# All FFN1 pairs of a parallel attention and FFN block take their last 64 features as stacks that pass DRAM

## The chip, the cores and the metric

One core of a Trainium2 chip runs the whole kernel. The metric is device time in microseconds (us) of one execution; lower is better. TensorE (PE) multiplies, VectorE (DVE) and ScalarE (ACT) work on the tiles between, GpSimd (POOL) does little arithmetic but issues loads and stores, and SyncE (SP) issues most of the other transfers. Each engine works through its own instructions in order; an instruction that must wait for data holds up everything behind it on the same engine.

## The reference

The input `x` has 2048 tokens of 576 features. Attention and FFN both read it and their results are added:

```python
def _A_ref(x, wqkv, wo):            # H = 32 heads of Dh = 18
    qkv = (x @ wqkv).reshape(B, S, 3, H, Dh)...
    idx = pos[:, None] - (jnp.arange(8) * 2)[None, :]      # 8 keys, every second token back
    logits = jnp.einsum("bhsd,bhswd->bhsw", q, kg) * Dh ** -0.5
    attn = softmax(where(idx >= 0, logits, -1e9))
    return einsum("bhsw,bhswd->bhsd", attn, vg)... @ wo
...
def _B_ref(x, w1, b1, w2, b2):      # F = 4608
    h = jnp.einsum("bsd,df->bsf", x, w1) + b1
    h = jnp.square(jax.nn.relu(h))
    return jnp.einsum("bsf,fd->bsd", h, w2) + b2
...
out = x + attention(layernorm(x)) + ffn(layernorm(x))
```

Everything is fp32. The kernel multiplies in PE's `fp32r` format and keeps fp32 accuracy by splitting each operand in a high part (ACT copies it, rounding) and a low part (DVE subtracts), and adding the three products high x high, low x high and high x low.

## The kernel before

The tokens are four blocks of 512, the FFN width is 36 tiles of 128, taken as 18 *pairs* (`p`). The first half (`s` = 0) does blocks 0 and 1, the second half (`s` = 1) blocks 2 and 3. A pair of FFN tiles against a pair of blocks is a 2 x 2 product, done as seven block products in the manner of Winograd: B11, T1, T2, T3, B21, B22 and T4 (`product` in `ffn_pair`). Each is six matmuls of 128 x 128 by 128 x 512 over the first 512 features: two chunks of 128, each with the three split products. `w1s` holds the split weights of a pair in two tiles (k = 0 and 1) with four product slots each; `combine_w1` makes T1, T2 and T4 weights on DVE, `w1_hi` and `w1_lo` split them in the first half and store them in DRAM (`w<-w1s`), and `w1_again` loads them back in the second half.

The last 64 features are treated apart, in one of two ways:

- *Unstacked* (`left`): the 64 features' high rows and low rows lie in one tile of 128 rows (`x4`), and two matmuls at four places of the pair add them, 8 a pair. All 18 pairs of the first half and pairs 0 and 1 of the second half do that. It needs a weight slot of its own, `LEFT`, the eighth in `w1s`.
- *Stacked*: the 64 features are two halves of 32 that go through the same seven products. High, low and high rows of a half lie on 96 partitions, beside weight rows high, high and low, so one matmul per product does all three split products: 7 a pair. Pairs 2 to 17 of the second half do that. Their weights are made per pair from a 256 KB load (`mb<-in_w1l`) by `left_weight_sums`, `left_weight_hi` and `left_weight_lo`; the stacks themselves are built on DVE and ACT while pairs 1 and 2 of the second half run (`stack_sums`, `stack_hi`, `one_stack` and their like).

The phases are: the QKV matmuls of blocks 0 and 1 (`q0`), the 18 pairs of the first half (`phase_a(0)`), a bridge of FFN2 work and the QKV of blocks 2 and 3 in 2 x 2 steps called quads (`phase_b0`), the 18 pairs of the second half (`phase_a(1)`), and the end (`phase_b1`). Within a pair, FFN2 matmuls of the pair before (L536) stand between the products. PE order in a pair: B11, T1, T2, T3, B21, B22, T4. `bc`, `ba`, `bb` are its three PSUM banks; T1 and later B22 go to `bc`, and B22 may start there once DVE has added T1's result to T3's (`r1[:, 1] = bc + u[:, 1]`).

Attention of each block runs on DVE in steps beside the pairs. `side(k)` takes up to k steps at a fixed place of the pair: after T1 three or so, after B22 two, after T4 two. A block and group (`b`, `g`) needs keys and queries, then values: keys and values are loads of 1296 KB into one of three `kv` tiles. `offer` lists the loads, `fetch` issues the next as long as a tile is free (`free`, less `kept_back` that it may not touch), and `release` gives a tile back, after the last `pr<-q,kv` for keys and after the last `q<-pr` for values. They are issued on POOL, in its order with the eight stores of a finished group (`o<-q`). The statistics of blocks 2 and 3 (`statistics`, L135 and the small operations behind it) are steps too; their input takes a `kv` tile, and they end with a store of 4 KB (`mr<-mr`) on SP.

In a pair, SP issues a store of r1 of the pair before (`h<-r`), two loads of w2 (`w2r<-in_w`) and between them a store of split w1, then in the first half a load of raw w1 (`w1r<-in_w`) for two pairs on. Each of these waits for the DVE instruction that frees its tile or makes its data.

## Time and profile before

| What | Value |
|---|---|
| Median of 3 runs | 1107.31 us (1107.31 to 1108.32) |
| The profiled execution | 1107.93 us, of which the span is 1106.2 us |
| QKV of blocks 0 and 1 | up to about 92 us |
| First half's pairs | from 92 to about 411 us, one every 17.68 us |
| FFN2, QKV of blocks 2 and 3 | to about 630 us |
| Second half's pairs | from 630 to about 952 us, one every 17.45 us where stacked |
| Bytes moved by DMA | 287.83 MB, 260 GB/s on average |

An execution outside the profile's span costs 1.7 us here. Busy time of an engine counts only if something else waits for it. In a row of the timeline the numbers are the start, the duration, the engine, the line, the operation, out<-in, and, in brackets, the time that the engine was idle just before and what ended that. In a row of transfers the last number is the median time from issue to landing. Chain lines give start, duration, engine, tile, line and the number of instructions merged.

### The profile page before, as it was taken

To read this page: it belongs to the slowest core of one execution; us is meant where nothing else is said; L and a number is where in the kernel's file an instruction comes from. 1 tells how busy PE (TensorE), PEld (TensorE's weight loads), DVE (VectorE), ACT (ScalarE), POOL (GpSimd) and SP (SyncE) were. 2 spreads that over 40 slices of the span, in tenths; PEclk is the share of its full clock that TensorE was granted. 3 is DMA by queue.
4 is the path that set the end of the run, shared out by engine and by line. 5 is a ranking of instruction groups with operands and counts; after the bars stand their busy time and mean duration, and the time that the engine had idled before them with its cause. 6 is when DMAs were issued, how large, how long until landed. Compare 5 with 4: busy or idle time off the path is not lost.

```text
span 1106.2 us, 13892 instructions
## 1 busy us (share of the span) xinstructions
PE 1096.8 (99%) x4950; PEld 925.2 (84%) x4950; DVE 912.0 (82%) x1223; ACT 575.0 (52%) x809; POOL 115.4 (10%) x219
## 2 busy tenths in 40 slices
PE   9999999999999999999999999999999999999998
PEld 7998888888888888888899887888888888888887
DVE  7696979897996979999979488978988789899654
ACT  5435666556566654455344355555555555533342
POOL 4000101020020100100010200202102021000100
PEclk9999999999999999999999999999999999999999
DMA  8956987889699686866755887768686785866752
GB/s 297 329 177 234 333 309 255 296 214 372 229 244 392 220 357 214 311 247 226 259 164 169 309 263 300 259 260 308 238 315 240 267 314 205 316 208 205 280 193 81
DMA packets 100279, 287.83 MB, mean 260 GB/s; under 512 B 13288, under 2 KB 41712, under 8 KB 85488
## 3 DMA queue, kind: packets, MB, share of 16 engines
q1 hardware_dynamic: 65280, 188.15, 49.1%
q0 software_dynamic: 10544, 52.14, 12.9%
q10 hardware_dynamic: 24384, 46.64, 12.6%
q8 instruction: 39, 0.64, 0.2%
q14 instruction: 32, 0.26, 0.1%
HBM read 205.14 MB, written 81.74 MB: 259 GB/s over the span
## 4 chain that ended last, share of the span: by engine, by line
PE 89%; DVE 5%; DMA 3%; ACT 1%; issue 1%; ACTq 0%; POOL 0%; DVEq 0%; POOLq 0%; SPq 0%
PE p L536 46%; PE p L629 31%; PE p L1041 5%; PE p L635 3%; DMA kvq<-st 2%; PE p L338 1%; PE p L1401 1%; PE p L1045 1%; DVE pr L108 1%; DMA kv<-kvq 1%; DVE lg L387 1%; DVE w1r L108 1%; DVE r L108 0%; PE p L1318 0%; DVE h L108 0%
## 5 line engine op out<-in xcount | busy, mean ns | idle before, releaser
L536 PE MATMUL p<-h,w2s 128*128 128x512 f32 x2066 | 491.4, 389 | 0.1
L536 PEld LDWEIGHTS p<-h,w2s 128*128 128x128 f32 x2066 | 387.5, 188 | 81.5 <-ACT h L642 0.6
L629 PE MATMUL p<-X,w1s 128*128 128x512 f32 x864 | 219.7, 389 | 1.2 <-DVE r L108 0.9
L629 PEld LDWEIGHTS p<-X,w1s 128*128 128x128 f32 x864 | 162.0, 188 | 35.6 <-DVE r L108 1.3
L509 ACT ACTIVATE w2s<-w2r 128x640 fp32r<-128x640 f32 x164 | 120.2, 735 | 116.1 <-PE p L536 87.6
L629 PE MATMUL p<-S,w1s 128*128 128x512 f32 x648 | 164.8, 390 | 1.5 <-ACT r L691 1.5
L108 DVE TENSOR_TENSOR w2s<-w2r,w2s 128x576 fp32r<-128x576 f32 x164 | 123.4, 753 | 40.6 <-ACT w2s L509 39.8
L629 PEld LDWEIGHTS p<-S,w1s 128*128 128x128 f32 x648 | 121.4, 188 | 27.4 <-ACT r L691 2.3
L415 POOL DMA_DIRECT2D o<-q x128 | 69.2, 605 | 584.8 <-DVE q L108 582.8
L638 ACT ACTIVATE r<-r,b1t 128x512 f32<-128x512 f32 x72 | 52.0, 723 | 126.9 <-DVE r L108 125.2
L387 DVE TENSOR_REDUCE lg<-pr 128x64 f32<-128x1152 f32 x64 | 86.5, 1352 | 1.5
L108 DVE TENSOR_TENSOR pr<-lg,kv 128x1152 f32<-128x1152 f32 x64 | 86.7, 1354 | 1.3
L108 DVE TENSOR_TENSOR pr<-q,kv 128x1152 f32<-128x1152 f32 x64 | 86.6, 1353 | 0.8
L108 DVE TENSOR_TENSOR pr<-pr 128x576 f32<-128x576 f32 (+1 forms) x128 | 77.5, 605 | 3.2
L646 ACT ACTIVATE r<-r 128x1024 f32<-128x1024 f32 x72 | 76.1, 1057 | 1.2
L108 DVE TENSOR_TENSOR h<-r,h 128x1024 fp32r<-128x1024 f32 (+3 forms) x46 | 51.8, 1136 | 27.0 <-ACT r L646 18.8
L108 DVE TENSOR_TENSOR r<-p,r 128x512 f32<-128x512 f32 (+1 forms) x77 | 52.9, 688 | 20.3 <-PE p L629 9.8
L108 DVE TENSOR_TENSOR w1s<-w1r,w1s 128x1024 fp32r<-128x1024 f32 (+1 forms) x42 | 50.3, 1198 | 16.5 <-ACT w1s L477 16.4
L691 ACT ACTIVATE r<-p 128x512 f32<-128x512 f32 x36 | 21.5, 597 | 70.9 <-PE p L629 70.5
L638 ACT ACTIVATE r<-p,b1t 128x512 f32<-128x512 f32 x72 | 48.3, 672 | 0.0
L108 DVE TENSOR_TENSOR h<-h 128x1024 fp32r<-128x1024 f32 x36 | 43.9, 1220 | 4.8 <-ACT h L938 4.6
L536 PE MATMUL p<-w1s,w2s 128*128 128x512 f32 x195 | 44.7, 389 | 0.0
(193 smaller groups left out, 1174.2 us busy)
## 6 DMA issues: line engine op xcount, KB each, us to landing
w2r<-in_w SPq DMA_DIRECT2D x144, 320.0 KB, 3.4
kv<-kvq POOLq DMA_DIRECT2D x29, 1296.0 KB, 9.4
w<-w1s SPq DMA_DIRECT2D x36, 1024.0 KB, 8.4
w1s<-w ACTq DMA_DIRECT2D x34, 1024.0 KB, 7.3
h<-r SPq DMA_DIRECT2D x36, 512.0 KB, 6.3
h<-h SPq DMA_DIRECT2D x36, 512.0 KB, 4.2
w1r<-in_w SPq DMA_DIRECT2D x18, 640.0 KB, 7.7
kvq<-st ACTq DMA_DIRECT2D x48, 216.0 KB, 3.2
```

The lines of the kernel that those rows point to most:

```text
L108: return nc.vector.tensor_tensor(out=out, in0=a, in1=b, op=op)
L338: nc.tensor.matmul(p[:, :QW], l, r, start=k == 0, stop=k == len(mm) - 1)
L387: nc.vector.tensor_reduce(out=lg[:, j * HG:(j + 1) * HG].rearrange("p a w -> p w a"), in_=pr.rearrange("p w (a d) -> p w a d", d=DH), axis ...
L415: nc.gpsimd.dma_start(rows[:, i], q[i * L:(i + 1) * L, :, a:z])
L509: nc.scalar.activation(w2s[stream[i]][:, :DE], raw2[i], AF.Copy)
L536: nc.tensor.matmul(yp[b][c], v, a, start=c not in yb[b], stop=c in last and c not in [o[0] for o in ops[i + 1:]], skip_group_check=True)
L629: nc.tensor.matmul(to, l, r, start=start and i == 0, stop=i == len(mm) - 1, skip_group_check=True)
L635: nc.tensor.matmul(to, weight(LEFT, k, f), v, start=False, stop=k == 1, skip_group_check=True)
L638: nc.scalar.activation(to, a, AF.Relu, bias=b1t[:, f:f + 1])
L646: nc.scalar.activation(r, r, AF.Square)
L691: nc.scalar.activation(u[:, 0], bb, AF.Copy)
L1041: nc.tensor.matmul(to, l[:, js], r, start=start and n == 0, stop=n == len(mm) - 1, skip_group_check=True)
```

## The change

All 36 pairs use the stacked form. `left` and the `LEFT` weight slot go, and the second w1 tile has three slots instead of four. The first half gets stacks as well (`left_x(0)`), and those of the second half are built earlier, while `phase_b0` runs. Building goes over all 128 partitions at once: four groups of 32 rows are four quarters of a block's tokens (`left_x`) or four pairs' weights (`left_w`). A high and a low version of 128 x 896 are made by one ACT and one DVE operation (`split_rows`), and twelve stores of 32 x 896 put them in the order of the stacks into DRAM, from where `load_stacks` fetches the stacks once a half and `load_left_weights(p + 1)` a pair's weights in every pair, behind T3.

The stack of the first half stays in one of the three `kv` tiles (with two small tiles beside it) until its pairs are done; `free` and `kept_back` are set for that. In the first pair of the second half, one row of quad output is stored later than before (`held`), behind the copy of T2's bank. In the first half `side` has other counts. The diff, cut to its core:

```diff
-T1, T3, B11, T2, B22, B21, LEFT, T4 = range(8)
+T1, T3, B11, T2, B22, B21, T4, LEFT = range(8)
 B12 = T2
 OA, OB = 3 * L, CG - 3 * L
+K3 = 3 * L
+NS = 7
+STACK = {T1: 0, B11: 1, B22: 2, B21: 3, T3: 4, T2: 5, T4: 6}
...
-    w1scr = [[dram.tile([P, 16 * P], F32, name=f"w1{p}{k}") for k in range(2)] for p in range(NP)]
-    xlscr = {b: dram.tile([2 * L, TB], F32, name=f"xl{b}") for b in (2, 3)}
+    w1scr = [[dram.tile([P, 2, 4 - k, 2 * P], F32, name=f"w1{p}{k}") for k in range(2)] for p in range(NP)]
+    xlscr = [dram.tile([2 * L, TB], F32, name=f"xl{b}") for b in range(NB)]
+    stscr = [dram.tile([K3, NS, TB], F32, name=f"stk{s}") for s in range(2)]
+    lwscr = [dram.tile([K3, NS * P], F32, name=f"lw{p}") for p in range(NP)]
...
+        if s == 0:
+            return
...
-        raw1[n] = sb.tile([P, 8, 2 * P], F32, name="w1r", bufs=2)
-        nc.sync.dma_start(raw1[n][:, B11:LEFT + 1], w1[n % NP])
+        raw1[n] = sb.tile([P, NS, 2 * P], F32, name="w1r", bufs=2)
+        nc.sync.dma_start(raw1[n][:, B11:B21 + 1], w1[n])
...
+    def open_w1(n, k):
+        w1s[n, k] = mt.tile([P, 2, 4, 2 * P], F32R, name="w1s", bufs=3)[:, :, :4 - k]
+        return w1s[n, k]
...
-    def open_left_weights():
-        t = sb.tile([P, 2, 7, P], F32R, name="w1r", bufs=2)
-        LW[0], LW[1] = t[:, 0], t[:, 1]
...
-    def left_weight_hi(p):
-        nc.scalar.activation(LW[p % 2], LR["w"], AF.Copy)
-    def left_weight_lo(p):
-        rows = slice(2 * L, P)
-        tt(LW[p % 2][rows], LR["w"][rows], LW[p % 2][rows].bitcast(F32), ALU.subtract)
-        load_left_weights(p + 1)
...
+    def split_rows(v, order, out):
+        lo, hi = v[:, :NS], v[:, NS:]
+        yield
+        nc.scalar.activation(hi.bitcast(F32R), lo, AF.Copy)
+        yield
+        tt(lo.bitcast(F32R), lo, hi, ALU.subtract)
+        for g in range(G):
+            for k, part in enumerate(order):
+                to = out(g, slice(k * L, (k + 1) * L))
+                if to is not None:
+                    nc.sync.dma_start(to, (hi, lo)[part][g * L:(g + 1) * L])
+        yield
...
+    def left_x(s):
+        v = rv.pop(s)
+        x = lambda k: v[:, STACK[k]]
+        tt(x(T3), x(B11), x(T1), ALU.subtract)
+        tt(x(T1), x(T1), x(T4), ALU.add)
+        tt(x(T2), x(T1), x(B11), ALU.subtract)
+        tt(x(B22), x(B21), x(T2), ALU.subtract)
+        yield from split_rows(v, (0, 1, 0), lambda g, rows: stscr[s][rows, :, g * P:(g + 1) * P])
+    def load_stacks(s, *tiles):
+        i = 0
+        for t in tiles:
+            n = min(t.shape[1], NS - i)
+            nc.sync.dma_start(t[:K3, :n].bitcast(F32), stscr[s][:, i:i + n])
+            for k, place in STACK.items():
+                if i <= place < i + n:
+                    ST[k] = t[:K3, place - i]
+            i += n
...
+    def left_w(i):
+        v = rv.pop(("w", i))
+        w = lambda k: v[:, STACK[k]]
+        tt(w(T3), w(B22), w(T1), ALU.subtract)
+        tt(w(T1), w(T1), w(B11), ALU.subtract)
+        tt(w(T2), w(B22), w(T1), ALU.subtract)
+        tt(w(T4), w(B21), w(T2), ALU.subtract)
+        yield from split_rows(v, (0, 0, 1), lambda g, rows: lwscr[G * i + g][rows].rearrange("r (s c) -> r s c", c=P)
+                              if G * i + g < NP else None)
...
     def load_left_weights(p):
-        if p < NP:
-            nc.sync.dma_start(LR["w"][:, 2:6], w1l[p])
-    def left_weight_sums():
-        r = LR["w"]
-        tt(r[:, 0:2], r[:, 3:5], r[:, 2:4], ALU.subtract)
-        tt(r[:, 3], r[:, 4], r[:, 0], ALU.subtract)
-        tt(r[:, 6], r[:, 5], r[:, 3], ALU.subtract)
-    def left_weight_hi(p):
-        nc.scalar.activation(LW[p % 2], LR["w"], AF.Copy)
-    def left_weight_lo(p):
-        rows = slice(2 * L, P)
-        tt(LW[p % 2][rows], LR["w"][rows], LW[p % 2][rows].bitcast(F32), ALU.subtract)
-        load_left_weights(p + 1)
+        src = lwscr[p].rearrange("r (s c) -> r s c", c=P)
+        tiles = ([sb.tile([P, NS, P], F32R, name="mb")] if p % 2 == 0 else
+                 [mt.tile([P, 4, P], F32R, name="x40"), mt.tile([P, 4, P], F32R, name="x41")])
+        i = 0
+        for t in tiles:
+            n = min(t.shape[1], NS - i)
+            nc.sync.dma_start(t[:K3, :n].bitcast(F32), src[:, i:i + n])
+            for k, place in STACK.items():
+                if i <= place < i + n:
+                    LW[p % 2, k] = t[:K3, place - i]
+            i += n
...
-            if stacked:
-                mm.append((LW[p % 2][:, STACK[slot]], ST[slot]))
+            mm.append((LW[p % 2, slot], ST[slot]))
...
-        def left(to, f, v):
-            if stacked:
+        def part(i):
+            if s:
                 return
-            for k in range(2):
-                nc.tensor.matmul(to, weight(LEFT, k, f), v, start=False, stop=k == 1, skip_group_check=True)
+            r = p // G + 1
+            if i == 0 and p % G == 1 and G * r < NP:
+                load_left_w(r, sb.tile([P, 2 * NS, P], F32, name="st"))
+            elif p % G == 2 and G * r < NP:
+                if i == 0:
+                    rv["of", r] = left_w(r)
+                next(rv["of", r])
...
+        part(0)
         if not first:
-            side(1 if p == 1 else 3 if s else 2 + p % 2, s == 1)
+            side(2 if not s and p % 4 == 2 else 3, s == 1)
...
         product(bb, T3, ss(3))
-        if first:
-            left(bc, 1, x4[b1])
+        if not last:
+            load_left_weights(p + 1)
...
             product(bc, B22, S4)
-            left(bc, 1, x4["d"])
-            if s and p == 1:
-                left_weight_lo(2)
-                one_stack_lo(T2)
-            elif not first:
+            part(1)
+            if not first:
                 side(2)
...
+        else:
+            release()
+            load_xf(2)
...
+            put = lambda: row_out(n, f, x, y)
+            held.append(put) if held is not None else put()
+        def row_out(n, f, x, y):
...
+                if (s, i) == (1, 0):
+                    load_stacks(1, *(sb.tile([P, 4, TB], F32R, name="w1r", bufs=2) for _ in range(2)))
+                    load_left_weights(0)
...
+        held = []
         def filler(i):
-            if i < 2:
-                quads(1, 1, [len(steps) - 2 + i])
+            if i == 0:
+                quads(1, 1, [len(steps) - 2], held)
+            if i == 0.5:
+                held.pop()()
             if i == 1:
-                load_left_rows()
-                LR["w"] = sb.tile([P, 7, P], F32, name="mb")
-                load_left_weights(2)
+                quads(1, 1, [len(steps) - 1])
...
+                free[0] -= 1
+                kept_back[0] = 0
+                load_left_x(0, kv_tile(2 * NS * P).rearrange("p (s t) -> p s t", t=P))
+            if r == 13:
+                load_left_weights(0)
...
+                load_stacks(0, sb.tile([P, 5, TB], F32R, name="kv", bufs=3), mt.tile([P, 1, TB], F32R, name="x4d"),
+                            sb.tile([P, 1, TB], F32R, name="xf"))
...
+    kept_back[0] = 1
```

**POOL, from the end of attention of block 0, group 3, to the next one's loads (around pair 8 of the first half).** `kv<-kvq_98` loads keys and later values of the next group, `q<-kvq_98` its queries, `o_100` and `o_101` are the outputs of the finished group, `mr` are the statistics of block 2. Before:

```order
L358 DMA q<-kvq_98 128x576
L360 DMA kv<-kvq_98 128x2592
L415 DMA o_100<-q 128x1x96 x4
L415 DMA o_101<-q 128x1x48 x4
L360 DMA kv<-kvq_98 128x2592
L144 TENSOR_TENSOR mr<-mr,half 128x1 x4
```

Now:

```order
L425 DMA o_100<-q 128x1x96 x4
L425 DMA o_101<-q 128x1x48 x4
L368 DMA q<-kvq_98 128x576
L370 DMA kv<-kvq_98 128x2592
L149 TENSOR_TENSOR mr<-mr,half 128x1 x4
L370 DMA kv<-kvq_98 128x2592
```

The loads of queries and keys stood ahead of the eight output stores and now stand behind them.

**DVE, at the end of block 2's statistics in the same pair.** `w2s`, `w1s` are weight splits, `r<-p,r` with the lower tile is the add that frees the bank for B22, `pr<-q,kv` the next group's first product with keys. Before:

```order
L135 BN_STATS st_2216<-kv 128x6 x2
L139 BN_AGGR mv<-st_2216 128x2
L158 COPY mr<-mv 128x1
L143 TENSOR_SCALAR mr<-mv 128x1
L108 TENSOR_TENSOR w2s<-w2r,w2s 128x576
L108 TENSOR_TENSOR w1s<-w1r,w1s 128x1024
L108 TENSOR_TENSOR w2s<-w2r,w2s 128x576
L108 TENSOR_TENSOR r_2274<-p_2189,r_2242 128x512
L108 TENSOR_TENSOR w1s<-w1r,w1s 128x1024
L108 TENSOR_TENSOR pr<-q,kv 128x1152
```

Now:

```order
L140 BN_STATS st_2347<-kv 128x6 x2
L144 BN_AGGR mv<-st_2347 128x2
L163 COPY mr<-mv 128x1
L148 TENSOR_SCALAR mr<-mv 128x1
L113 TENSOR_TENSOR pr<-q,kv 128x1152
L113 TENSOR_TENSOR w2s<-w2r,w2s 128x576
L113 TENSOR_TENSOR w1s<-w1r,w1s 128x1024
L113 TENSOR_TENSOR w2s<-w2r,w2s 128x576
L113 TENSOR_TENSOR r_2414<-p_2318,r_2379 128x512
L113 TENSOR_TENSOR w1s<-w1r,w1s 128x768
```

The product with the new keys has moved ahead of the weight splits and of the add, by five places.

**SP, from the store of block 2's statistics (`mr_109`) on, in the same pair.** `h_178` and its like are stores of r1, `w_129` of split w1, and `x_2408`, `x_2409` are the two tiles that take the left weights of pair 9 from DRAM. Before:

```order
L162 DMA mr_109<-mr 128x8x1
L150 DMA kv<-in_x 128x2304
L656 DMA h_156<-r_2101 128x1024
L499 DMA w2r<-in_w 128x640
L483 DMA w_129<-w1s 128x2048
L499 DMA w2r<-in_w 128x640
L467 DMA w1r<-in_w 128x1280
```

Now:

```order
L167 DMA mr_109<-mr 128x8x1
L682 DMA h_178<-r_2231 128x1024
L511 DMA w2r<-in_w 128x640
L496 DMA w_129<-w1s 128x2048
L511 DMA w2r<-in_w 128x640
L619 DMA x_2408<-lw_162 96x512
L619 DMA x_2409<-lw_162 96x384
L477 DMA w1r<-in_w 128x1024
```

The load of block 3's rows (`kv<-in_x`) has left this place, since no `kv` tile is free for it there; the two loads of left weights have come in behind the second w2r.

118 lines of the change are left out of this document (37 added, 81 removed).

## The prediction

> **What bounds the kernel now.** I read the page first: busy time, then the chain that ended last.
>
> ```profile
> PE 1096.8 (99%) x4950; PEld 925.2 (84%) x4950; DVE 912.0 (82%) x1223; ACT 575.0 (52%) x809; POOL 115.4 (10%) x219
> PE 89%; DVE 5%; DMA 3%; ACT 1%; issue 1%; ACTq 0%; POOL 0%; DVEq 0%; POOLq 0%; SPq 0%
> ```
>
> PE is busy 99% of the span and carries 89% of the chain. So a matmul less is time won, and any other engine costs time only where it makes PE wait. Next I read the chain in order of time inside the pair loop, at the same matmuls of successive pairs: two lines from the first half, two from the second.
>
> ```profile
> 118.37 2.72 PE p L629 x12
> 136.05 2.72 PE p L629 x12
> 759.81 3.17 PE p L629 x14
> 777.26 3.17 PE p L629 x14
> ```
>
> Twelve matmuls take 2.72 us, 0.227 each. The pair takes 17.68 us in the first half and 17.45 in the second: the difference is one matmul, 8 unstacked against 7 stacked ones for the last 64 features. PE never rests inside such a pair, so it is the limit there. Last came PE's waits, for the little that is not matmul.
>
> **Matmuls removed.** The list of PE groups by shape shows the unstacked ones (L635) and the stacked ones (the others):
>
> ```profile
> L635 PE MATMUL p<-x,w1s 128*128 128x512 f32 x120 | 37.0, 390 | 0.0
> L635 PE MATMUL p<-x4d,w1s 128*128 128x512 f32 x40 | 12.3, 389 | 0.0
> L629 PE MATMUL p<-w1r 128*128 128x512 f32 x64 | 24.9, 389 | 0.0
> L629 PE MATMUL p<-x,w1r 128*128 128x512 f32 x32 | 12.4, 389 | 0.0
> L629 PE MATMUL p<-x4d,w1r 128*128 128x512 f32 x16 | 6.2, 389 | 0.0
> ```
>
> 160 unstacked are 20 pairs of 8; 112 stacked are 16 pairs of 7. All 36 at 7 saves 20 matmuls; the stream's step of 0.227, not the modelled 389 ns, is the price: **-4.5 us**.
>
> **Stalls removed.** Three PE waits fall where the second half starts and its stacks and first weights are built:
>
> ```profile
> 628.59 0.53 ACT L1050 ACTIVATE st<-p 128x432 f32<-128x432 f32 x1 [4.46 <-DMA kvq<-st]
> 630.21 1.65 PE L629 MATMUL p<-S,w1s 128*128 128x512 f32 x6 [0.85 <-ACT r L691]
> 666.02 1.20 PE L629 MATMUL p<-X,w1s 128*128 128x512 f32 x4 [0.93 <-DVE r L108]
> 680.16 1.66 PE L629 MATMUL p<-S,w1s 128*128 128x512 f32 x6 [0.70 <-ACT r L691]
> ```
>
> At 628.59 ACT sat behind a store of quad output; the change puts that output (`held`) behind the copy that PE needs. At 666 and 680 DVE and ACT were late with stack building that now lies earlier, beside the 62 us of FFN2 and quads before. The idle times sum to 2.5; each hides 0.16 more (389 ns modelled end, 227 ns step): **-3.0** (0 to -3.0). What comes late next there is the stacks' own trip through DRAM, counted as a rival. The per-pair stack weights leave DVE and ACT of the second half too:
>
> ```profile
> L108 DVE TENSOR_TENSOR w1r<-mb,w1r 64x896 fp32r<-64x896 f32 x16 | 17.4, 1090 | 4.5 <-ACT w1r L595 4.1
> ```
>
> That is 1.09 us a pair beside 17.45 of PE: 0 to the time, since PE does not wait there.
>
> **One attention buffer less in the first half.** The stacks sit in one of three `kv` tiles. Before, the next block's keys were fetched early (198.10); now only two tiles are free, and the load of keys stands in POOL behind eight output stores and the query load. The views are POOL's and DVE's timelines around pair 8 (PE's pair starts at 234.42):
>
> ```profile
> 198.10 0.54 POOL L360 DMA_DIRECT2D kv<-kvq  x1 [5.96 <-DVE pr L108]
> 231.54 0.31 DVE L108 TENSOR_TENSOR q<-pr 128x144 f32<-128x144 f32 x1
> 232.14 2.16 POOL L415 DMA_DIRECT2D o<-q  x4 [33.50 <-DVE q L108]
> 240.53 0.75 DVE L108 TENSOR_TENSOR w2s<-w2r,w2s 128x576 fp32r<-128x576 f32 x1
> 241.70 1.23 DVE L108 TENSOR_TENSOR w1s<-w1r,w1s 128x1024 fp32r<-128x1024 f32 x1 [0.43 <-ACT w1s L477]
> 244.15 0.69 DVE L108 TENSOR_TENSOR r<-p,r 128x512 f32<-128x512 f32 x1 [0.46 <-ACT r L723]
> 246.24 1.35 DVE L108 TENSOR_TENSOR pr<-q,kv 128x1152 f32<-128x1152 f32 x1
> 246.72 1.52 PE L629 MATMUL p<-X,w1s 128*128 128x512 f32 x6
> ```
>
> The queue of transfers, by issue to landing, in 231 to 252, and (last line) the one load of keys issued at 309.30, when its stores had landed:
>
> ```profile
> kv<-kvq POOLq DMA_DIRECT2D x1, 1296.0 KB, 9.4
> w2r<-in_w SPq DMA_DIRECT2D x2, 320.0 KB, 15.2
> o<-q POOLq DMA_DIRECT2D x4, 48.0 KB, 6.0
> mr<-mr SPq DMA_DIRECT2D x1, 4.0 KB, 10.6
> kv<-kvq POOLq DMA_DIRECT2D x1, 1296.0 KB, 6.6
> ```
>
> The stores start at 232.14, the first lands 6.0 later, the query load takes 0.6 of issue: keys go out at 238.7 and land 6.6 to 9.4 later, 245.3 to 248.1. The new order puts the first product with them (`pr<-q,kv`) right behind the statistics, at 240.53. DVE therefore waits 4.8 to 7.6 us, and behind it stand w2s, w1s, w2s and the add that frees PE's bank for product B22: 1.35 + 0.75 + 1.23 + 0.76 + 0.69 = 4.8. The add ends at 250.1 to 252.9; PE wanted the bank at 246.72. **PE waits 3.4 to 6.2.**
>
> **The load of left weights in the same pair.** They now come by SP, behind the pair's second w2r, and the next pair's seventh matmul needs them: 234.42 + 17.45 + 6 x 0.227 = 253.2. Ahead of them on SP stands the 4 KB store of statistics:
>
> ```profile
> 241.71 0.39 SPq L162 DMA_DIRECT2D mr<-mr  x1
> 243.10:252.00 8.90, 8.90 (x41) 7.38 (x40) 8.12 (x8) 5.06 (x7) 0.00 (x0) 1.00 1.04 95
> 252.00:260.80 8.80, 8.80 (x41) 7.28 (x40) 8.34 (x10) 5.56 (x8) 0.53 (x1) 1.00 0.99 397
> ```
>
> In these stretches the last two numbers are the DMA share and GB/s. While that store is in flight (to 252.3) the engines are full and move 95 GB/s; afterwards 397; the w2r loads behind it took 15.2 to land. Behind it, in SP's order, come 512, 320, 1024, 320 and 344 KB, 2.6 MB or 6.5 us: left weights at 258.8, up to 3.3 later if the values' 1296 KB share the engines. Against 253.2 that is 5.6 to 8.9. It overlaps the bank's wait instead of adding to it, so the two together cost 3.4 (transfers free) to 8.9; I take **+6.0**, near the end that both rows of this pair support.
>
> Three pairs later the same comes again for blocks 1 and 3, but more work stands before the product: a 0.9 us split of left weights and the last attention step, then three statistics. By the same durations keys go out 8.7 us into the pair and land at 15.3 to 18.1; DVE wants them at 14. Its wait of 1.3 to 4.1 reaches PE only beyond the slack of the next bank, 0 to 3; the left weights go out 11.6 us in and share the engines with the keys, 0 to 4 late. I take **+2.0** (0 to 7).
>
> **Left weights elsewhere.** Their nearest relative is the raw load of the second half, one place earlier on SP:
>
> ```profile
> 768.78 0.33 SPq L586 DMA_DIRECT2D mb<-in_w1l  x1
> mb<-in_w1l SPq DMA_DIRECT2D x1, 256.0 KB, 10.5
> mb<-in_w1l SPq DMA_DIRECT2D x16, 256.0 KB, 6.6
> ```
>
> By the median of all 16 (6.6) it would land 775.4, in time for 777.26 + 1.36 = 778.6; this one landed 779.3, 0.7 late, which did no harm since a pair lay between landing and use. In the change nothing lies between. I take four such pairs of the second half at 0.4, **+1.5** (0 to 9), and **+0.7** (0 to 4) for pairs of the first half with attention loads; a pair's stall moves the later ones along, so they do not pile up.
>
> **Small terms.** DVE gains five operations in every fourth pair of the first half, where an attention pair was nearly full already:
>
> ```profile
> 216.60:234.30 17.70, 17.70 (x80) 14.66 (x79) 17.09 (x29) 10.51 (x14) 2.16 (x4) 1.00 0.60 209
> ```
>
> DVE has 17.09 of 17.70 there, less what leaves it (a narrower w1 split); three such pairs give +0.4 (0 to 3). The opening gets the first stacks and left weights under QKV matmuls that fill PE; 0 (-0.5 to +2). The 12 stores of each four pairs stand on SP ahead of a row store that nothing waits for: 0.
>
> **Sum:** -4.5 - 3.0 + 6.0 + 2.0 + 1.5 + 0.7 + 0.4 = +3.1. The profiled execution took 1107.9 (span 1106.2 and 1.7 outside it), 0.6 above the median of 1107.3: 1111.0 profiled, **1110.4** as a median.
>
> **A rule to weigh.** For a load of keys this trace has 6.6 and 9.4 us. The Trainium skill (DMA: Bandwidth & Descriptors, Anatomy of one DMA) states about 2.0 us plus bytes over 436 GB/s, which is an estimate of 5.0 us here; both rows stand above it. By it the keys would land at 243.7 and PE's bank wait would be 1.8.
>
> The rivals use one more row, of all loads of w2:
>
> ```profile
> w2r<-in_w SPq DMA_DIRECT2D x144, 320.0 KB, 3.4
> ```
>
> **Rivals.** (1) *Not slower:* the 4 KB store gets out of the way, because the keys' wait on DVE delays the w2r loads anyway and the left weights with them meet idle engines; then only the bank's wait is left, at its low end 3.4, and the rest of the loads arrive by their medians. -7.5 + 3.4 = -4.1: 1103.2. For it speaks the 6.6 row; against it 95 GB/s in 243 to 252. It decides at 256.6: left weights landing sooner than that cost nothing. (2) *Quick transfers:* a load takes a fixed part and its bytes at the 397 GB/s of 252 to 261. The row of w2 loads gives the fixed part, 3.4 - 0.8 = 2.6; keys then take 2.6 + 3.3 = 5.9, land at 244.6 and leave a bank's wait of 2.7, and nothing else is late: -7.5 + 2.7 = -4.8: 1102.5. Against it stand both rows of keys. The Trainium skill's formula above is another form of this; by it the time would be 1101.6. (3) *Left weights late again and again:* bounds of 9 and 4 instead of 1.5 and 0.7: +10.8 more, 1121. For it the 10.5 row, against it the median. (4) *The start of the second half keeps its stalls,* because stacks and left weights pass DRAM among stores that made ACT wait 4.46: -4.5 + 10.6 = +6.1: 1113.4.
>
> **How the numbers follow.** Forecast 0.45 (own range 1107 to 1117), rivals 0.27, 0.07, 0.10, 0.11. The range must leave out no more than 2 in 10: 1102 to 1118. About 0.2%, 2.2 us, is what a measurement can tell: faster means below 1105.1, slower above 1109.5. Faster: rivals 1 (0.25 of it) and 2, and 0.01 of the forecast, 0.33. Slower: 0.25 of the forecast, rivals 3 and 4 but for 0.01, 0.45. Same: the rest, 0.22.
>
> **What would show it.** Twenty matmuls fewer and pairs of 17.45 from the first on; no PE wait at the start of the second half; in pair 8 a DVE wait of 5 to 8 us on the keys at `pr<-q,kv` and a PE wait of 3 to 6 on its add; at pair 9's seventh matmul a PE wait on left weights. If PE's waits in pairs 8 to 12 sum below 4, I am wrong on the transfers.

## The result, and the profile after

| | before | after |
|---|---|---|
| Median | 1107.56 us (6 runs, 1107.31 to 1108.32) | 1166.13 us (6 runs, 1163.19 to 1171.03) |
| Profiled execution, its span | 1107.93, 1106.2 us | 1163.19, 1161.2 us |
| Up to the first FFN1 matmul | 92.28 | 96.44 |
| First half's 18 pairs, first to last FFN1 matmul | 316.51 | 344.88 |
| From their end to the second half's first FFN1 matmul | 212.97 | 223.61 |
| Second half | 328.06 | 340.12 |
| From the last pair to the end | 156.40 | 156.11 |

The ratio is 1.0532, 95% interval 1.0504 to 1.0559: 58.6 us slower, where +3.1 was forecast and 1118 was the end of the range. The direction had the largest chance, 0.45; the size was missed entirely. The stages above differ by +4.2, +28.4, +10.6, +12.1 and -0.3, together the 55.0 between the spans.

The page after, busy time and the chain that ended last:

```profile
PE 1114.5 (96%) x4930; PEld 928.1 (80%) x4930; DVE 879.8 (76%) x1181; ACT 560.8 (48%) x793; POOL 116.8 (10%) x221
PE 69%; DMA 17%; DVE 8%; ACT 2%; issue 2%; SPq 1%; POOL 0%; ACTq 0%; DVEq 0%; POOLq 0%
```

The twenty matmuls are gone (4950 to 4930). PE's busy time rose by 17.7 us all the same, and transfers went from 3% of the chain to 17%. What PE waited for, in total, times and longest:

```profile
PE p L649 <- DMA x<-lw: 11.2, 3, 5.8
PE p L649 <- DMA mb<-lw: 11.0, 5, 8.5
PE p L649 <- DMA w1s<-w: 6.9, 1, 6.9
PE p L649 <- DVE r L113: 4.9, 3, 3.1
PE p L649 <- ACT w1s L490: 3.8, 1, 3.8
```

`x` and `mb` are the two places of the left weights (odd and even pairs). Eight of the loads came late, for 22.2 us; `w1s<-w` is the first split weight of the second half. Before, no wait of PE on a transfer stands in this view, and its longest was 2.1. The chain in order of time gives the places:

```profile
145.70 3.21 PE p L649 x14
...
260.68 12.38 DMA x<-lw
273.11 3.57 PE p L649 x8
319.78 16.41 DMA mb<-lw
336.23 3.78 PE p L649 x8
...
647.88 17.00 DMA w1s<-w
664.93 3.35 PE p L649 x7
```

A load that took 12 to 17 us stands ahead of each of these three stops of PE. Two smaller things are in these rows as well: 14 matmuls of an undisturbed pair take 3.21, where the kernel before had 3.17, and eight behind a stop take 3.57 or 3.78, where 0.227 each would be 1.8.

**The stop costs more than itself.** The stretch around 336 in the table of windows (from and to, PE, PEld, DVE, ACT and POOL busy, granted clock, DMA share, GB/s):

```profile
324.00:328.00 4.00, 3.75 (x17) 2.76 (x15) 2.41 (x3) 0.42 (x1) 0.00 (x0) 1.00 1.04 426
328.00:332.00 4.00, 0.00 (x0) 0.00 (x0) 3.66 (x4) 2.99 (x4) 0.00 (x0) 0.86 1.01 349
332.00:336.20 4.20, 0.00 (x0) 0.00 (x0) 4.06 (x6) 0.00 (x0) 0.00 (x0) 0.50 1.01 283
336.20:340.00 3.80, 3.77 (x9) 2.99 (x10) 1.78 (x2) 2.17 (x3) 0.00 (x0) 0.50 0.95 195
340.00:344.00 4.00, 4.00 (x17) 3.21 (x16) 0.08 (x1) 0.16 (x1) 0.00 (x0) 0.86 0.81 60
```

The granted clock falls to 0.50 while PE rests and stays there for the next 3.8 us: 9 matmuls against 17 in a like stretch. The Trainium skill (TensorE: Matmul & The Clock Gate, Part 1, What's actually happening) states this as a gate: half clock after an idle window of about 3.4 us, full clock again after about as long a busy one. The trace agrees. Over all matmuls that start between 90 and 1006 us, the steps from one start to the next that are longer than 0.62 us add 43.2 us beyond 0.227 each. Those of 0.30 to 0.62 add 14.0: 10.9 at half clock, and 3.1 at full clock, in small waits and in the step right behind a stop. Together with the matmuls of 96 rows (below), that is why PE is busier with fewer matmuls.

**Pair 8, as it was forecast.** DVE's and then PE's timeline there:

```profile
251.94 0.14 DVE L148 TENSOR_SCALAR mr<-mv 128x1 f32<-128x1 f32 x1
256.39 1.36 DVE L113 TENSOR_TENSOR pr<-q,kv 128x1152 f32<-128x1152 f32 x1 [4.30 <-DMA kv<-kvq]
...
260.13 0.68 DVE L113 TENSOR_TENSOR r<-p,r 128x512 f32<-128x512 f32 x1
```

```profile
260.87 1.66 PE L649 MATMUL p<-X,w1s 128*128 128x512 f32 x6 [3.13 <-DVE r L113]
...
273.11 0.80 PE L649 MATMUL p<-kv,x 96*128 96x512 f32 x1 [5.77 <-DMA x<-lw]
```

The keys hold DVE for 4.3 us, the add that frees the bank comes late, and PE waits 3.13: the mechanism of the forecast. The second row is the left weights, 5.77 more; the two together are 8.9, the upper end that the forecast gave for this pair. The queue that carried them (253 to 275), issue to landing in the last number:

```profile
x<-lw SPq DMA_DIRECT2D x1, 192.0 KB, 12.4
x<-lw SPq DMA_DIRECT2D x1, 144.0 KB, 12.2
mr<-mr SPq DMA_DIRECT2D x1, 4.0 KB, 13.7
```

### The profile page after: what moved, and what is told of

Same layout as the page of the kernel before. It is cut to its first block, busy times and chain, and to the rows that moved or that the text cites. A ratio compares the mean times of both kernels' runs of the same rounds, so it can differ in the third digit from the quotient of the medians.

```text
span 1161.2 us, 13998 instructions
## 1 busy us (share of the span) xinstructions
PE 1114.5 (96%) x4930; PEld 928.1 (80%) x4930; DVE 879.8 (76%) x1181; ACT 560.8 (48%) x793; POOL 116.8 (10%) x221
## 3 DMA queue, kind: packets, MB, share of 16 engines
q10 hardware_dynamic: 26560, 42.19, 11.5%
## 4 chain that ended last, share of the span: by engine, by line
PE 69%; DMA 17%; DVE 8%; ACT 2%; issue 2%; SPq 1%; POOL 0%; ACTq 0%; DVEq 0%; POOLq 0%
PE p L548 30%; PE p L649 27%; DMA mb<-lw 5%; PE p L1040 4%; PE p L348 4%; DMA x<-lw 3%; DMA w1s<-w 3%; DVE pr L113 2%; DMA w2r<-in_w 2%; DVE w2s L113 1%; DMA kvq<-st 1%; PE p L1410 1%; DVE h L113 1%; DVE r L113 1%; DVE w1s L113 1%
## 5 line engine op out<-in xcount | busy, mean ns | idle before, releaser
L548 PE MATMUL p<-h,w2s 128*128 128x512 f32 x2066 | 496.8, 392 | 1.6 <-DVE w2s L113 1.2
L649 PE MATMUL p<-X,w1s 128*128 128x512 f32 x864 | 224.4, 395 | 15.8 <-DMA w1s<-w 6.9
L649 PE MATMUL p<-S,w1s 128*128 128x512 f32 x648 | 170.2, 399 | 0.0
L649 PEld LDWEIGHTS p<-S,w1s 128*128 128x128 f32 x648 | 125.1, 193 | 27.5 <-ACT st L1053 0.6
L113 DVE TENSOR_TENSOR w1s<-w1r,w1s 128x1024 fp32r<-128x1024 f32 (+2 forms) x42 | 45.4, 1082 | 24.6 <-ACT w1s L490 20.8
```

Source lines behind the costliest of these rows:

```text
L113: return nc.vector.tensor_tensor(out=out, in0=a, in1=b, op=op)
L548: nc.tensor.matmul(yp[b][c], v, a, start=c not in yb[b], stop=c in last and c not in [o[0] for o in ops[i + 1:]], skip_group_check=True)
L649: nc.tensor.matmul(to, l, r, start=start and i == 0, stop=i == len(mm) - 1, skip_group_check=True)
```

## The experiments

All are edits of the kernel after, except the two whose name begins with before. Differences are between medians; the ratio is to the kernel before, run on the same chip.

| Run | Median us | Ratio (95%) |
|---|---|---|
| two_loads_only | 1139.71 | 1.0288 (1.0268 to 1.0309) |
| early_load | 1139.49 | 1.0286 (1.0266 to 1.0307) |
| wide_store | 1168.97 | 1.0552 (1.0517 to 1.0587) |
| early_keys_later | 1149.93 | 1.0379 (1.0349 to 1.0410) |
| earliest_keys_later | 1141.98 | 1.0306 (1.0276 to 1.0336) |
| early_w2_later | 1138.55 | 1.0277 (1.0247 to 1.0306) |
| early_w1_by_act | 1141.50 | 1.0303 (1.0273 to 1.0333) |
| early_stacks_too | 1129.27 | 1.0191 (1.0161 to 1.0221) |
| before_held | 1107.64 | 0.9996 (0.9987 to 1.0006) |
| before_96_rows | 1110.62 | 1.0025 (1.0015 to 1.0034) |
| early_full_rows | 1138.37 | 1.0275 (1.0181 to 1.0369) |
| all_moves | 1127.58 | 1.0176 (1.0131 to 1.0221) |
| all_moves_rows_by_fill | 1120.01 | 1.0108 (1.0081 to 1.0134) |
| all_moves_three_tiles | 1123.84 | 1.0143 (1.0123 to 1.0163) |
| all_moves_rows_sides | 1110.50 | 1.0026 (1.0016 to 1.0037) |
| all_moves_rows_sides_2 | 1111.47 | 1.0035 (1.0024 to 1.0045) |
| all_moves_rows_sides_3 | 1117.86 | 1.0084 (1.0062 to 1.0106) |

### The loads of left weights: away, or earlier

**two_loads_only** loads them for the first two pairs of each half only; the later pairs multiply by these again.

```diff
         product(bb, T3, ss(3))
-        if not last:
+        if first:
             load_left_weights(p + 1)
```

> The changed kernel, but each half loads the left weights of its pairs 0 and 1 only and uses them again in all later pairs, so those products are left with the wrong weights; 32 loads of 344 KB are gone. Theory of late loads: the waits of PE on left weights (22 us in the profile, and the slow clock after the long ones, together some 35) go; what is left are the start of each half, the wait on keys in pair 8 and the dear rows: about 1125 to 1135. Rival (the queue is simply full, and any other load takes their place as the late one): above 1145.

**early_load** keeps all of them, but issues each ahead of the pair's two w2 loads.

```diff
         if before:
             next(before, None)
+        if not first and not last:
+            load_left_weights(p + 1)
...
         product(bb, T3, ss(3))
-        if not last:
+        if first:
             load_left_weights(p + 1)
```

> The changed kernel with the load of the next pair's left weights issued ahead of the pair's w2 loads instead of behind T3, some 6 us earlier, with nothing left out. Theory of late loads: a load that is issued before the statistics' store and the w2 loads lands in time, so nearly all of the waits on left weights go and the time is within 5 us of the kernel that loads only two: 1125 to 1140. Rival (full queue): PE waits on left weights stay above 12 us in sum and the time stays above 1150.

Both give the same, 26.4 and 26.6 us less than the change. So, within the 3.3 us between the two runs of early_load, the loads cost nothing by being there, and their price lay in the place on SP. PE's waits in early_load:

```profile
PE p L649 <- DMA w1s<-w: 10.3, 1, 10.3
PE p L649 <- DVE r L113: 6.1, 4, 3.9
```

No wait on left weights is left. The 22.2 us of waits account for most of the gain. The half clock behind three of them is a further part, 6.3 by the steps of the change, and PE's wait on `w1s`, 10.3 instead of 6.9, takes some of it back.

### The 4 KB store, and the keys

**wide_store** writes the statistics as 128 runs of 32 bytes instead of runs of 4, and reads them back with strides.

```diff
-  nc.sync.dma_start(mrscr[b].rearrange("n p -> p n"), mr.rearrange("p k j -> p (k j)"))
+  nc.sync.dma_start(flat(mrscr[b], 0, [2 * NJ, P], 2 * NJ), mr.rearrange("p k j -> p (k j)"))
```

> The changed kernel with the statistics of blocks 2 and 3 stored in 128 runs of 32 bytes instead of 1024 of 4, and read back in that order. Theory of the 4 KB store: the store lands in 3 us instead of 14 to 23, the left weights of pair 9 land 8 us earlier, those of pair 12 some 5: 12 to 20 us less, 1146 to 1154. Rival (the attention loads fill the queue whatever the store does): less than 5 us.

The queue in pair 8 (245 to 275), then around pair 11 (319 to 345):

```profile
x<-lw SPq DMA_DIRECT2D x1, 192.0 KB, 6.3
x<-lw SPq DMA_DIRECT2D x1, 144.0 KB, 5.4
mr<-mr SPq DMA_DIRECT2D x1, 4.0 KB, 4.9
```

```profile
mr<-mr SPq DMA_DIRECT2D x1, 4.0 KB, 16.0
```

In pair 8 the store lands in 4.9 instead of 13.7 and the left weights behind it in 6.3: there the narrow store was the cause. In pair 11 little changed: PE still waits 7.9 for left weights there, against 8.5. In the change itself they were issued at 319.78, ahead of the store at 322.67. This is the change's queue in 319 to 337:

```profile
mb<-lw SPq DMA_DIRECT2D x1, 336.0 KB, 16.4
...
mr<-mr SPq DMA_DIRECT2D x1, 4.0 KB, 23.0
```

With the DMA share near 1 at 283 to 426 GB/s (the windows above) the queue is full there. The time as a whole says little about the store, since the strided normalisation cost more itself: DVE spends 17.6 us on it in the bridge instead of 9.6, and the bridge grew by 12.7.

**early_keys_later** takes one attention step less in pair 8, so that the product with the keys comes behind the bank's add.

```diff
-            side(2 if not s and p % 4 == 2 else 3, s == 1)
+            side(2 if not s and (p % 4 == 2 or p == 8) else 3, s == 1)
```

> The kernel of the early load, with two attention steps instead of three behind T1 of pair 8 of the first half, so that the product with the newly loaded keys stands behind the weight splits and the add for B22, as before. Theory of the keys: PE's wait of 4.3 us in pair 8 goes, and with it the slow clock after it, some 2 us: 1133 to 1136. Rival (the wait moves to what DVE does next, since the keys are late anyway): pair 8 stays above 21 us and the time above 1138.

**earliest_keys_later** adds to that the loads of left weights as the first thing of a pair.

```diff
         before = prev.pop("finish", None)
+        if not first and not last:
+            load_left_weights(p + 1)
         product(ba, B11, ...)
```

> The load of the next pair's left weights as the first thing of a pair, ahead of the statistics' store in SP's order, and two attention steps instead of three in pair 8. The run with the early load and two steps had that load behind the statistics' store, and PE waited 8.8 us for it. Theory of SP's order: ahead of the store both waits go, on keys and on left weights, and pair 8 falls from 23.6 to below 19: 1132 to 1135. Rival (engines full with keys and values, whatever the order): pair 8 above 22 and the time above 1138.

The bank's wait of pair 8 went in both. But the first of them has this on PE's timeline, and the second the row behind it:

```profile
270.95 0.80 PE L649 MATMUL p<-kv,x 96*128 96x512 f32 x1 [8.84 <-DMA x<-lw]
```

```profile
331.49 2.93 PE L649 MATMUL p<-X,w1s 128*128 128x512 f32 x6 [3.19 <-DVE r L113]
```

Without the bank's wait PE was at the left weights sooner, and they came later: issued at 252.7 behind the narrow store as in early_load, they landed after 18.2 us instead of 14.5, among transfers that SP could now issue earlier. The time is 10.4 us above early_load. With the load at the head of the pair that is gone, but the wait on attention's add came back four pairs later. The late keys were worth little alone; a stop that is removed shows the next.

### The opening and the start of the second half

The change's first FFN1 matmul came 4.2 us late. ACT's timeline, then PE's:

```profile
94.36 0.53 ACT L340 ACTIVATE st<-p 128x432 f32<-128x432 f32 x1 [1.94 <-DMA kvq<-st]
```

```profile
96.44 0.79 PE L649 MATMUL p<-X,w1s 128*128 128x512 f32 x1 [3.84 <-ACT w1s L490]
```

ACT stood behind a store of QKV output, with 1.3 MB of stack loads in flight, and split the first weights late (at 95.33). **early_w2_later** (on early_load) puts three w2 loads behind the first w1 split there.

```diff
-                for n in range(3):
-                    load_w2(n)
                 combine_w1(0)
...
                 w1_lo(0, r - 23)
+                if r == 24:
+                    for n in range(3):
+                        load_w2(n)
```

> The kernel of the early load, with the three w2 loads of the opening issued behind the first w1 split instead of ahead of it. Theory of the opening: ACT's wait for a QKV store behind 1.3 MB of stacks and 1 MB of w2 is what makes the first w1 split late; 1 MB less is 2 to 3 us: the first FFN1 matmul comes at 94 to 95 instead of 97.3, PE does not rest long enough to fall to the slow clock, and the time falls by 3 to 5 us, to 1135 to 1137. Rival (the stacks alone hold ACT): under 1 us.

The first FFN1 matmul starts at 95.29 instead of 97.26, but a new wait of 1.7 on ACT appears at 108.6, and the medians differ by 0.9, within the spread of early_load's two runs.

**early_w1_by_act** (on early_load) issues the first two `w1s` loads of the second half on ACT's queue, so that they pass the stack loads on SP's.

```diff
-                    w1_again(NP, 0, nc.sync)
+                    w1_again(NP, 0)
```

> The kernel of the early load, with the first two loads of split w1 of the second half issued on ACT's queue, where T1's copies of the last quad stand, instead of on SP behind quad stores and the stacks. Theory of the SP order: the first load leaves some 5 us earlier, and PE's wait of 10.3 us at the start of the second half falls to 3 to 6: 1132 to 1136. Rival (the engines are full there with 3.4 MB of attention loads, 1.4 MB of stacks and 2 MB of w1, whatever the order): the wait stays above 8, and the time above 1137.

```profile
652.78 0.77 PE L649 MATMUL p<-w1r,mb 96*128 96x512 f32 x1 [7.51 <-DMA mb<-lw]
```

The wait moved to the next load of the same jam, and nothing was won. The queue of the change in 640 to 665 shows it:

```profile
kv<-kvq POOLq DMA_DIRECT2D x1, 1296.0 KB, 13.1
w1s<-w SPq DMA_DIRECT2D x1, 1024.0 KB, 17.0
...
kv<-o POOLq DMA_DIRECT2D x1, 768.0 KB, 15.8
```

The `w1s` were issued at 647.88, some 10 us ahead of their use, where the kernel before had 11.5 (610.24 and 621.76); there they landed in 5.0. Here 1.3 MB of stacks went out at 646.4 to 646.9, and attention's loads at 646.9 and 648.5. **early_stacks_too** adds to early_w1_by_act that the stacks and first left weights are loaded some 20 us sooner, among the quads.

```diff
+            if k and not half and (s, i) == (2, 1):
+                load_stacks(1, *(...))
+                load_left_weights(0)
...
-                if (s, i) == (1, 0):
-                    load_stacks(1, *(...))
-                    load_left_weights(0)
```

> The kernel of the early load, with the second half's stacks and first left weights loaded one quad round (some 30 us) earlier, and its first w1 by ACT's queue. Theory of a full queue at that place: with 1.8 MB out of the last 12 us of the bridge the first w1 lands in 5 to 8 us, and PE's wait at the start of the second half (10.3, and 7.5 in the run with w1 by ACT) falls below 2: 1125 to 1129. Rival (attention's loads alone fill it): the wait stays above 6, and the time above 1135.

It takes 10.2 us less than early_load. The first `w1s` now land in 5.2, and PE's longest wait there is:

```profile
643.70 0.49 PE L688 MATMUL p<-X,w1s 128*128 128x512 f32 x1 [0.82 <-ACT st L1055]
```

**before_held** puts the change's `held` alone into the kernel before: the row of quad output is stored behind the copy of T2's bank.

```diff
+            put = lambda: row_out(n, f, x, y)
+            held.append(put) if held is not None else put()
...
+            if i == 0.5:
+                held.pop()()
```

> The kernel before with nothing but the late quad output: the first row of the last two is held back behind the copy of T2's bank in the second half's first pair. Theory (ACT sits behind a store's landing at 628.59 and PE waits 0.85 us for its copy): that wait goes, 0.7 to 1.2 us less than before. Rival (ACT waits at the next store just the same): within 0.3 us.

```profile
632.62 0.73 PE L635 MATMUL p<-x,w1s 128*128 128x512 f32 x2 [0.95 <-DMA w1s<-w]
```

The wait on `r` at 630 is gone, and 2.4 us later PE waits as long for `w1s`. The time is the same within 0.13%. The two waits at 666 and 680 are still there, since this kernel builds its stacks as before.

### Operands of 96 rows

An undisturbed pair took 17.64 us instead of 17.45. In the change a stacked matmul has 96 rows; in the kernel before it had 128, of which 32 were zero. **before_96_rows** gives those of the kernel before 96:

```diff
-  mm.append((LW[p % 2][:, STACK[slot]], ST[slot]))
+  mm.append((LW[p % 2][:3 * L, STACK[slot]], ST[slot][:3 * L]))
```

> The kernel before, with the 112 stacked matmuls of the second half on the 96 rows that hold data instead of 128 rows of which 32 are zero. Theory of rows (a matmul of 96 rows among those of 128 costs about 27 ns more, as the calm pairs of the changed kernel, 17.64 us, suggest): the second half's pairs go from 17.45 to 17.64, the time up by 16 x 0.19 = 3.0 us. Rival (the 0.19 comes from something else in the changed kernel, such as its transfers): pairs stay at 17.45, time within 0.5 us of before.

It is 2.8 us slower, for 112 such matmuls: 25 ns each. **early_full_rows** (on early_load) goes the other way, with zero rows that pass DRAM:

```diff
-            nc.sync.dma_start(t[:K3, :n].bitcast(F32), src[:, i:i + n])
+            nc.sync.dma_start(t[:, :n].bitcast(F32), src[:, i:i + n])
...
-                    LW[p % 2, k] = t[:K3, place - i]
+                    LW[p % 2, k] = t[:, place - i]
```

> The kernel of the early load, with stacks and left weights on 128 rows, 32 of them zero in the stacks (four stores more for four pairs and 448 instead of 336 KB a load). Theory of rows: calm pairs go from 17.64 to 17.45 in both halves, 36 x 0.19 = 6.8 us less, about 1132.5. Rival (the longer loads and stores come late in their turn and give it back): PE waits on left weights of over 2 us, and 1136 or more.

Its two runs lie 8.7 us apart, so the time decides nothing. Its trace has calm pairs at 17.45, but the loads, a third larger, were late again:

```profile
PE p L650 <- DMA mb<-lw: 4.4, 2, 2.2
```

### The moves together

**all_moves** joins earliest_keys_later, early_w1_by_act, early_stacks_too and early_w2_later.

> All of these moves together: left weights first in a pair, two steps in pair 8, the second half's stacks a round earlier with w1 by ACT's queue, w2 behind the first w1 split. Theory (each place has a queue of its own to clear, and the gains add): 12 at the start of the second half, 6 in pair 8, 2 in the opening: 1117 to 1122. Rival (a wait removed comes back at the next full place): above 1128.

Only 1.7 less than early_stacks_too, which is within the 4.1 between its own two runs. **all_moves_rows_by_fill** adds 128 rows, with POOL writing the 32 zero rows into each tile instead of a larger load:

```diff
+            nc.gpsimd.memset(t[K3:, :n].bitcast(F32), 0.0)
             nc.sync.dma_start(t[:K3, :n].bitcast(F32), src[:, i:i + n])
...
-                    LW[p % 2, k] = t[:K3, place - i]
+                    LW[p % 2, k] = t[:, place - i]
```

> All moves together, and stacks and left weights on 128 rows, the last 32 filled with zeros by POOL in every pair, with no byte more by DMA. Theory of rows: 36 x 0.19 = 6.8 us below all moves on 96 rows (1127.6), so 1119 to 1122, with calm pairs of 17.45. Rival (POOL's fills hold up the attention stores and loads behind them): above 1124.

It won 7.6 (the runs of all_moves lie 4.1 apart, those of this kernel 7.6); undisturbed pairs take 17.45 instead of 17.64, which makes 6.8 for 36. A form of it that filled the stacks' rows but not those of the left weights, all_moves_full_rows, gave no time. The chain of all_moves, and of this kernel, at one place of a first-half pair:

```profile
142.81 3.21 PE p L649 x14
```

```profile
142.44 3.17 PE p L651 x14
```

Of these 14 matmuls two are stacked: 0.04 for two, near the 25 ns each of before_96_rows.

**all_moves_three_tiles** (on all_moves) gives attention its third `kv` tile back. Five of the first half's seven stacks are not loaded; their products use the two others.

```diff
-  load_stacks(0, sb.tile([P, 5, TB], F32R, name="kv", bufs=3), ...)
+  load_stacks(0, mt.tile([P, 1, TB], F32R, name="x4d"), sb.tile([P, 1, TB], F32R, name="xf"))
+  for k, place in STACK.items():
+      ST[k] = ST[T1 if place % 2 == 0 else B11]
+  release()
```

> All moves together on 96 rows, but the first half reads its stacks from the two small tiles alone (five of seven products are left with another product's stack; 960 KB less are loaded in the opening) and so gives the third kv tile back to attention. Theory of the tile: PE's waits on DVE in pairs 8, 11 and 12 go, keys are fetched early again, attention runs ahead, and the first half falls from 328.5 to 320 to 322; 1117 to 1121. Rival (the waits on DVE come from its load of work, not from keys): first half above 326.

3.7 less, which is within the 4.1 between the runs of all_moves. PE's wait on DVE's `r` falls from 5.9 to 2.3, but two waits on left weights (2.2) appear and one on ACT's `r` grows from 2.0 to 3.3. The first half takes 327.5 instead of 328.5, so the rival held: no more than 4 of the 20 us that all_moves still lacked hang on the tile.

**all_moves_rows_sides** (on all_moves_rows_by_fill) takes one attention step less at the first place of pairs 1, 11 and 12 too, where PE had waited for DVE.

```diff
-            side(2 if not s and (p % 4 == 2 or p == 8) else 3, s == 1)
+            side(2 if not s and (p % 4 == 2 or p in (1, 8, 11, 12)) else 3, s == 1)
```

> All moves on 128 rows, and two attention steps instead of three behind T1 also in pairs 1, 11 and 12 of the first half. Theory of the keys (the product with late keys stands ahead of the add that frees PE's bank, now in pair 12): the wait of 4 us in pair 12 and those of pairs 1 and 11 go, 6 to 9 us below the run without it. Rival (a step put off comes back in the next pair): less than 3 us.

9.5 less: 1110.5. Most of it is pair 12, where in all_moves_rows_by_fill DVE had waited for keys:

```profile
322.58 1.36 DVE L113 TENSOR_TENSOR pr<-q,kv 128x1152 f32<-128x1152 f32 x1 [4.07 <-DMA kv<-kvq]
```

PE then waited 3.28 for the add, half clock followed, and the pair took 23.77; now it takes 17.45. Pairs 1 and 11 give 1.5 together. Another 2.1 lie in pair 0, which the edit does not touch, and pair 15 loses 1.0.

**all_moves_rows_sides_2** does the same in pair 7, where one of two waits of 0.7 was left, and **all_moves_rows_sides_3** also changes the last place in pairs 3, 5, 9, 10 and 13.

```diff
-            side(2 if not s and (p % 4 == 2 or p in (1, 8, 11, 12)) else 3, s == 1)
+            side(2 if not s and (p % 4 == 2 or p in (1, 7, 8, 11, 12)) else 3, s == 1)
...
-        side(2, False)
+        side(3 if not s and p in (3, 5, 9, 10, 13) else 2, False)
```

The first two lines are sides_2, and sides_3 has all four. With 3 instead of 2 the last place of those pairs takes one step more. So attention there runs sooner, not later as the expectation of sides_3 says, and that theory is left untested. The expectation of sides_2 names pair 14 too; the other wait of 0.7 was in pair 15, and the edit leaves it as it is.

> As all_moves_rows_sides, with the second side step taken in pair 7 and in pair 14 as well. Theory: the two stops of TensorE on VectorE's r that are left in the first half (steps of about 1.1 us in pairs 7 and 14 there) go, 1.5 to 2.5 us in all, so the run takes 1107.5 to 1109.5 us, within 0.2% of the kernel before. Rival: what is put off is only done later, the wait on ScalarE's h at the start of the second half (2.1 us) grows and the time stays at 1110 to 1112.

> As all_moves_rows_sides_2, with the last side step of first-half pairs 3, 5, 9, 10 and 13 put off as well. Theory, if stops on VectorE's attention steps are what is left between this and the kernel before: another 1 to 2 us less than all_moves_rows_sides_2, 1106 to 1108 us, at or under the kernel before. Rival: attention now runs late for the bridge, TensorE waits at the start of the second half, and the run is 1 to 4 us slower than all_moves_rows_sides_2.

PE's waits in sides_2, then in sides_3:

```profile
PE p L548 <- ACT h L873: 2.6, 1, 2.6
...
PE p L651 <- ACT r L708: 2.1, 1, 2.1
```

```profile
PE p L651 <- DVE r L113: 2.3, 4, 0.7
...
PE p L651 <- DMA mb<-lw: 2.0, 1, 2.0
```

In sides_2 the rival held: the wait of pair 7 is gone, but the wait on ACT's `h` at the start of the second half grows from 2.1 to 2.6, one of 2.1 on ACT's `r` appears in pair 0, which the edit does not touch, and the time stays. sides_3, 7.4 above all_moves_rows_sides, loses 5.6 in the first half, to DVE's `r` and left weights again; its rival had named the start of the second half. No version of the change came under the kernel before.

## Why the prediction was wrong

The gains by step add up to 55.6 of the 58.6 us: 26.6 (left weights ahead of w2), 10.2 (stacks and first loads of the second half earlier), 1.7 (keys and w2 later, loads still earlier), 7.6 (128 rows) and 9.5 (attention steps moved). Each is what it won on top of those before it; in another order the parts would differ, since stops hide one another, and the 1.7 is within the spread of its runs.

**The step that failed most is the price of the left weights.** For everything that they touch the sum held 10.2 us (6.0, 2.0, 1.5 and 0.7), PE's wait on the bank in pair 8 included. Issuing them ahead of w2, and nothing else, won 26.6. They had been priced by the median landing of a load of their kind and by the slack left in their pair. What decided was the tail: eight loads of 35, issued behind the w2 loads, came late (two of them took 12.4 and 16.4 to land), for 22.2 us of PE's waits and 6.3 of half clock behind these. Term by term:

- **Removed matmuls, -4.5.** The count is right, and at 128 rows a first-half pair takes 17.45. The first half of all_moves_rows_sides still takes 317.32 against 316.51, though 16 x 0.227 = 3.6 are gone: its steps over 0.30 add 5.3 us beyond 0.227 each (2.4 over 0.62, and 2.8 below, 1.6 of that at half clock), against 1.0 before. The gain exists, and the stops take it.
- **Stalls removed, -3.0: wrong in its sign.** before_held shows that removing the wait at 630 only uncovers the next. The two at 666 and 680 did go: the change has no wait of PE on DVE or ACT in the first three pairs of the second half. But the stacks' own trip through DRAM, left to rival 4, was worth +10.2. Not ACT's wait decided there, as that rival had it: the stacks were loaded at the moment at which `w1s` and attention's loads wanted the queue.
- **Pair 8, +6.0.** The mechanism held: DVE waited 4.30 on the keys (4.8 to 7.6 forecast), PE 3.13 on the bank (3.4 to 6.2) and 5.77 on left weights. 8.9 in all is the upper end of 3.4 to 8.9; the middle was taken.
- **Pairs 11 and 12, +2.0** (0 to 7). The wait on the keys did not reach PE here; it did in all_moves_rows_by_fill, for 6.3 with the half clock behind it. The left weights landed after 16.4 us in a full queue and stopped PE for 8.48; 0 to 4 had been allowed for them.
- **Left weights elsewhere, +1.5 and +0.7.** Of the 22.2 us of waits, 14.3 are those of the loads issued in pairs 8 and 11, so 7.9 fell elsewhere: 6.9 in the second half (1.5 taken, bound 9) and 1.1 in the first (0.7 taken, bound 4). The price came from a median of 6.6, and the median was not wrong: 7.6 for `mb`, 6.2 and 6.1 for `x` in the change. Eight loads of 35 came late. Rival 3 had the mechanism, with a chance of 0.10.
- **The opening, 0.** It was +4.2: the stack loads were in flight when ACT had to store QKV output. How much of it they cause is open: with w2 out of the way, 960 KB less of them bring the first FFN1 matmul from 93.89 (all_moves) to 93.50 only (all_moves_three_tiles).
- **DVE's fuller pairs, +0.4.** The row of 17.09 busy in 17.70 had shown little room. PE's waits on DVE's add in pairs 1 and 7 are 1.32 and 0.48 in the change, and moving the steps of pairs 1 and 11 won 1.5.
- **Not in the sum at all:** the half clock after a stop (10.9 us of slow steps, none before) and the 96 rows (7.6). The rows stood in the diff, as `:K3`, and were read as a change of place only.

Of the markers, twenty matmuls fewer and the waits in pairs 8 and 9 came as stated (DVE's a little shorter); pairs of 17.45 from the first on, and no wait at the second half's start, did not.

Open: the last 2.6 us between all_moves_rows_sides and the kernel before. By the traces, whose spans differ by 3.4, the opening has 2.0 more, the first half 0.8 and the bridge 1.4, the rest 0.8 less; no run closed that. What the half clock cost by itself was not measured apart from the stops that cause it.

## What to carry to other kernels

A load that is both issued and used within a pair must be priced by the tail of the queue it joins, in that stretch and in that engine's order, not by the median of its kind: issue it earlier, away from the large loads, and ahead of whatever waits for something else. A long stop of PE costs its length and, as a rule, a stretch at half clock behind it. When a wait is to be removed, ask first what would be late next: several single moves here won nothing, since the next late thing stood right behind.

## What the runs showed of the hardware

- **Half clock after a rest.** The length of PE's rest alone does not decide. Rests of 3.04, 3.13 and 3.27 us (wide_store, the change, all_moves_three_tiles) were followed by six matmuls in 1.65 or 1.66, as usual; one of 3.19 (earliest_keys_later) by six in 2.93, like those of 6.94 and 10.30. In all_moves_rows_by_fill a rest of 1.76 was enough:

```profile
107.28 2.62 PE L651 MATMUL p<-S,w1s 128*128 128x512 f32 x6 [1.76 <-ACT r L708]
```

  What decides is how the rest falls into fixed stretches of 3.41 us. In the change the clock is at half from 95.40 to 102.22, 269.48 to 276.30, 330.92 to 341.16, 662.01 to 668.84 and 986.28 to 993.10, which is two, two, three, two and two times 3.41 us, and all these times lie whole multiples of 3.41 apart; it is so in all 19 traces. Here are such stretches around the rest of 1.76 in all_moves_rows_by_fill, then around the one of 3.13 in the change:

```profile
104.24:107.65 3.41, 1.65 (x9) 1.21 (x8) 0.00 (x0) 1.65 (x3) 0.41 (x1) 1.00 0.96 342
107.65:111.06 3.41, 3.41 (x10) 2.65 (x9) 1.29 (x2) 1.75 (x3) 0.00 (x0) 0.50 0.24 77
```

```profile
255.82:259.24 3.42, 1.92 (x9) 1.25 (x7) 2.85 (x3) 0.07 (x1) 0.00 (x0) 1.00 1.29 149
259.24:262.65 3.41, 1.78 (x8) 1.47 (x9) 3.41 (x5) 1.30 (x2) 0.00 (x0) 1.00 1.02 143
262.65:266.06 3.41, 3.41 (x17) 2.79 (x16) 3.38 (x4) 1.05 (x2) 0.00 (x0) 1.00 0.79 241
```

  The rest of 1.76 lies in one stretch and leaves PE 1.65 busy there; the one of 3.13 is shared by two, with 1.92 and 1.78. Over all traces, a stretch at full clock with less than 1.5 us of busy PE was always followed by one at half clock (42 of them), and one with more than 1.65 never; in between it went both ways. (Full clock reads 0.95 in early_stacks_too, 1.00 in the others.) This fits a window that runs freely, as the Trainium skill has it (TensorE: Matmul & The Clock Gate, Part 1, What's actually happening). But the Trainium skill speaks of an idle window there, and here one in which PE was busy for up to 1.65 of 3.41 was enough.
- **96 rows among 128.** A stacked matmul of 96 rows cost some 25 ns more than one filled up with 32 zero rows, at equal columns: +2.8 us for 112 of them, and -7.6 for 252 when the rows were filled. Why, no run here shows.
- **A 4 KB store in runs of 4 bytes** took 13.7 us to land, and the loads behind it 12; in runs of 32 bytes it took 4.9 at the same place, and the loads behind it 6.3 and 5.4. In the full queue of pair 11 the narrow form took 23.0 and the wide one 16.0.
